# Local attention probabilities of batches 3 to 7 turned by 32x32 block transfers and VectorE instead of TensorE, in a new order of steps

## The chip, the cores and the metric

The kernel runs on one core of a Trainium2 chip. The metric is the device time of one execution in microseconds; the time before is 602.74 us, the median of three runs (602.57 to 603.37). One further execution was taken with the hardware profiler on; its page and trace are what is read below. Engines are named as in the profile: PE is TensorE (matmul), PEld its weight loads, DVE is VectorE, ACT is ScalarE, POOL is GpSimd, SP is SyncE, which here only issues DMA transfers.

## The reference

Eight batches, eight heads, 576 positions, head dimension 64. Two attentions are added and the sum goes through a feed-forward layer:

```python
# pooled: q, k, v averaged over groups of 4 positions, full softmax attention on 144 positions,
# the result repeated 4 times
out_up = np.repeat(sm_attn(q_d, k_d, v_d), 4, axis=2)
# local: each position sees only positions closer than 4
mask = np.abs(pos[:, None] - pos[None, :]) < 4
scores = np.where(mask, scale * np.matmul(q, k.transpose(0, 1, 3, 2)), -1e9)
out_local = np.matmul(softmax(scores), v)
x = (out_up + out_local) as 4608 tokens x 512
# feed-forward
h = x @ w_in                      # 512 -> 1024
solu = h * softmax(h)
ln = (solu - mean) / sqrt(var + 1e-6) * g_ln
return ln @ w_out                 # 1024 -> 512
```

Everything is computed in float32; the weights come as float64 and are converted on the chip.

## The kernel before

**Feed-forward.** The 4608 tokens are 36 tiles of 128. Both matmuls of a tile are done in a split of each operand into a high and a low part, three products per block: `ffn_in` (L770) issues 24 matmuls of 128x512, `ffn_out` (L888) another 24. `xhl` makes the parts of the input (`xh` on ACT at L919, `xl` on POOL at L922). Between the two matmuls stand the maximum (DVE, L778), the exponential (ACT, L782), the product with its sum (DVE, L785), the subtraction of the mean (ACT, L807), the square sum (ACT, L822) and some small POOL steps. To turn the 128x1024 result so that its columns lie on partitions, it is stored to a scratch tensor in memory (`u`, L813), read back in 32-row blocks (`v`, four transfers at L845), and transposed in 32x32 blocks by DVE (L866). ACT then makes `uh` (L872) and POOL (DVE for the last tiles) makes `ul` (L874).

**Local attention.** A batch's 576 positions are covered by ten windows of 64 rows, handled two at a time: five units (`Local`, u = 0 to 4) in each of eight batches, 40 in all. In `by_tensor`, which all 40 use, a unit goes through eleven steps: the scores of four head pairs (PE, L614: 16 products of 64x64, in the profile two records each), the mask added on the way out of PSUM into `pl` (DVE, L632), the row maximum (DVE, L637), its subtraction (POOL, L639), the exponential (ACT, L641), the row sum and its reciprocal (DVE, L644 and L648), the multiplication by it (POOL, L650), four 128x128 transposes of `pl` into PSUM (PE, L660), their copy to `plT` in SBUF (ACT, L663), the products with the values `vw` (PE, L670), and the write into `x` (L496 ACT for batches 1 to 7, L498 DVE for batch 0). `vw` comes by four transfers per unit (L264).

A second method, `by_blocks` (L515), is in the text and unused, because `ON_TENSOR = 8`. It lays `pl` out so that a later 32x32 block transpose is enough: eight transfers of 32 rows by 1 KB bring the blocks to their places in `plT` (L569), one DVE transpose of 128x512 turns them (L575), and the products read `plT` directly. Its values come by two transfers per unit, and its row sum is followed by a small DVE addition of 1e-9 (128x8).

**Pooled attention.** Per batch four head pairs (`Pooled`): scores (PE, L696), maximum (DVE, L703), exponentials (ACT, L711), reciprocal (DVE, L718), multiplication (POOL, L720), transposes (PE, L731), two copies (ACT L738; DVE L743 from batch 2 on, ACT before), products (PE, L752), addition to `x` (DVE, L498). The pooled values are summed on POOL (`pooled_vsum`, L434 and L437).

**Order.** All work is cut into 2099 numbered steps (generators that yield between instructions, collected in `plan`). `ORDER` at the top of the file lists the numbers in the order in which the steps are emitted, and each engine executes its own in that order. A tile that a step writes or reads makes the engines wait for one another; a DMA transfer makes the engine that issues it wait for its data. The first stretch also holds the conversion of the weights (`Weights`, L323 to L362, mainly DVE) and 24 pairs of matmuls on zeros (`keep_clock`).

Of the kernel before, what the change touches and what calls it, by code (L numbers as in the profile page):

```python
# [10 lines left out]
F32 = mybir.dt.float32  # L11
# [118 lines left out]
def pooled_local_attention_then_solu_ffn(  # L130
# [11 lines left out]
    P = 128  # L142
# [358 lines left out]

    ON_TENSOR = 8

    class Local:

# [534 lines left out]
```

## Time and profile before

| | |
|---|---|
| median of three runs | 602.74 us |
| profiled execution: its own time / its span | 602.74 us / 601.0 us |
| busy PE / PEld | 574.8 / 447.1 us |
| busy DVE / ACT / POOL | 396.5 / 361.8 / 375.6 us |
| share of the 16 DMA engines' time | 63.3% |
| moved | 94.34 MB in 203,913 packets |

The span runs from the first to the last instruction; the 1.74 us by which the execution's time exceeds it lie around it. "Busy" is the time in which at least one instruction of the engine ran, so overlapping instructions count once. A group's row gives the number of instructions, their busy time, the mean duration of one in ns, then the idle time just before them and who ended it. The chain of waits is followed back from the last instruction and gives each piece of the span to the engine or line that set it.

### The profile page before, as it was taken

To read this page: it belongs to the slowest core of one execution; us is meant where nothing else is said; L and a number is where in the kernel's file an instruction comes from. 1 tells how busy PE (TensorE), PEld (TensorE's weight loads), DVE (VectorE), ACT (ScalarE), POOL (GpSimd) and SP (SyncE) were. 2 spreads that over 40 slices of the span, in tenths; PEclk is the share of its full clock that TensorE was granted. 3 is DMA by queue.
4 is the path that set the end of the run, shared out by engine and by line. 5 is a ranking of instruction groups with operands and counts; after the bars stand their busy time and mean duration, and the time that the engine had idled before them with its cause. 6 is when DMAs were issued, how large, how long until landed. Compare 5 with 4: busy or idle time off the path is not lost.

```text
span 601.0 us, 15341 instructions
## 1 busy us (share of the span) xinstructions
PE 574.8 (96%) x5912; PEld 447.1 (74%) x5912; DVE 396.5 (66%) x692; ACT 361.8 (60%) x800; POOL 375.6 (62%) x553
## 2 busy tenths in 40 slices
PE   6889789899999999999999999999999999999996
PEld 3666557677777777787877777777777878788785
DVE  5989999869747677766856767737655533643541
ACT  3758866577745566566664854657465655553443
POOL 2576668867784778678574777656786767332221
PEclk8979999899999999999999999999999999999999
DMA  8999776687769767766878567847416623124230
GB/s 231 238 251 254 140 183 146 164 178 162 195 144 189 171 167 186 170 148 175 190 151 201 143 173 182 185 114 195 97 59 188 146 89 114 63 88 151 96 123 35
DMA packets 203913, 94.34 MB, mean 157 GB/s; under 512 B 162496, under 2 KB 192704, under 8 KB 203840
## 3 DMA queue, kind: packets, MB, share of 16 engines
q1 hardware_dynamic: 203840, 93.37, 63.3%
q8 instruction: 46, 0.75, 0.6%
q14 instruction: 27, 0.22, 0.1%
HBM read 65.54 MB, written 27.79 MB: 155 GB/s over the span
## 4 chain that ended last, share of the span: by engine, by line
PE 75%; POOL 6%; DVE 5%; ACT 4%; SPq 4%; DMA 3%; issue 3%; POOLq 0%; DVEq 0%
PE o L888 31%; PE h L770 27%; PE xp L670 3%; PE plt L660 3%; PE po L752 3%; PE sc L614 2%; DMA qm<-in_q_dram 2%; SPq L245 2%; PE pdt L731 2%; PE sd L696 2%; POOL pl L639 2%; DMA v<-u 1%; SPq L264 1%; POOL pd L720 1%; DVE w L334 1%
## 5 line engine op out<-in xcount | busy, mean ns | idle before, releaser
L888 PE MATMUL o<-wo_h,uh 128*128 128x512 f32 x288 | 117.9, 409 | 0.8 <-ACT uh L872 0.7
L770 PE MATMUL h<-wi_h,xh 128*128 128x512 f32 x288 | 116.3, 404 | 0.6 <-DVE e L785 0.6
L770 PE MATMUL h<-wi_h,xl 128*128 128x512 f32 x288 | 114.3, 397 | 1.3 <-POOL xl L922 1.3
L888 PE MATMUL o<-wo_l,uh 128*128 128x512 f32 x288 | 114.5, 398 | 0.0
L770 PE MATMUL h<-wi_l,xh 128*128 128x512 f32 x288 | 114.1, 396 | 0.0
L874 POOL TENSOR_TENSOR ul<-v,uh 128x512 fp32r<-128x512 f32 x58 | 74.4, 1288 | 19.7 <-ACT uh L872 7.7
L778 DVE TENSOR_REDUCE nmx<-h 128x1 f32<-128x1024 f32 x36 | 43.9, 1219 | 63.8 <-PE h L770 63.8
L888 PE MATMUL o<-wo_h,ul 128*128 128x512 f32 x288 | 79.1, 396 | 0.4 <-DVE ul L874 0.4
L782 ACT ACTIVATE e<-h,nmx 128x1024 f32<-128x1024 f32 x36 | 40.0, 1112 | 51.0 <-DVE nmx L778 51.0
L888 PEld LDWEIGHTS o<-wo_h,uh 128*128 128x128 f32 x288 | 54.6, 190 | 15.6 <-ACT uh L872 1.4
L770 PEld LDWEIGHTS h<-wi_h,xl 128*128 128x128 f32 x288 | 54.2, 188 | 15.2 <-POOL xl L922 2.1
L770 PEld LDWEIGHTS h<-wi_h,xh 128*128 128x128 f32 x288 | 54.2, 188 | 14.8 <-issue 1.0
L888 PEld LDWEIGHTS o<-wo_h,ul 128*128 128x128 f32 x288 | 54.2, 188 | 14.0 <-DVE ul L874 0.8
L770 PEld LDWEIGHTS h<-wi_l,xh 128*128 128x128 f32 x288 | 54.3, 189 | 12.2
L888 PEld LDWEIGHTS o<-wo_l,uh 128*128 128x128 f32 x288 | 54.5, 189 | 11.8
L922 POOL TENSOR_TENSOR xl<-x,xh 128x512 fp32r<-128x512 f32 (+1 forms) x40 | 47.1, 1183 | 18.6 <-ACT xh L919 17.4
L807 ACT ACTIVATE e<-e,nmu 128x1024 f32<-128x1024 f32 x35 | 40.1, 1146 | 28.2 <-POOL nmu L790 28.1
L785 DVE SCALAR_TENSOR_TENSOR e<-h,e 128x1024 f32<-128x1024 f32 x36 | 43.7, 1214 | 19.9 <-ACT e L782 19.9
L650 POOL TENSOR_TENSOR pl<-pl,rsl 128x512 f32<-128x512 f32 x40 | 42.1, 1055 | 20.7 <-DVE rsl L648 18.2
L866 DVE STREAM_TRANSPOSE v<-v 128x512 f32<-128x512 f32 x70 | 46.3, 688 | 12.5 <-DMA v<-u 12.5
L872 ACT ACTIVATE uh<-v 128x512 fp32r<-128x512 f32 x70 | 42.9, 623 | 14.9 <-DVE v L866 11.0
L639 POOL TENSOR_TENSOR pl<-pl,mxl 128x512 f32<-128x512 f32 x40 | 41.8, 1052 | 9.0 <-DVE mxl L637 4.6
(95 smaller groups left out, 1076.1 us busy)
## 6 DMA issues: line engine op xcount, KB each, us to landing
u<-e SPq DMA_DIRECT2D x35, 512.0 KB
v<-u SPq DMA_DIRECT2D x140, 128.0 KB
vw<-in_v_dram SPq DMA_DIRECT2D x160, 64.0 KB
vs<-in_v_dram SPq DMA_DIRECT2D x32, 288.0 KB
out_dram<-osb SPq DMA_DIRECT2D x36, 256.0 KB
qm<-in_q_dram SPq DMA_DIRECT2D x96, 72.0 KB
km<-in_k_dram SPq DMA_DIRECT2D x96, 72.0 KB
w<-in_moe_w_out_dram SPq DMA_DIRECT2D x8, 512.0 KB
```

The source lines that it names most:

```text
L639: nc.gpsimd.tensor_tensor(out=pl, in0=pl, in1=max_bc, op=ALU.subtract)
L650: nc.gpsimd.tensor_tensor(out=pl, in0=pl, in1=rs.unsqueeze(3).broadcast_to([P, NPR, 2, W]), op=ALU.mult)
L770: nc.tensor.matmul(hps[:, n, :], src[:, cc, :], wt[:, cc, n * 512:(n + 1) * 512], start=(cc == 0 and src is xh and wt is wi_h), stop=(cc = ...
L778: nc.vector.tensor_reduce(out=nmx, in_=hf, op=ALU.max, axis=AX.X, negate=True)
L782: nc.scalar.activation(e, hf, AF.Exp, bias=nmx, scale=1.0, accum_out=se)
L785: nc.vector.scalar_tensor_tensor(out=e, in0=hf, scalar=1.0, in1=e, op0=ALU.mult, op1=ALU.mult, accum_out=su)
L807: nc.scalar.activation(e, e, AF.Identity, bias=nmu, scale=1.0)
L866: nc.vector.transpose(vg, vg)
L872: nc.scalar.activation(uh, tp, AF.Copy)
L874: (nc.vector if v is None or i in LATE else nc.gpsimd).tensor_tensor(out=ul, in0=tp, in1=uh.bitcast(F32), op=ALU.subtract)
L888: nc.tensor.matmul(o, src[:, j, :], wt[:, 4 * g + j, :], start=(g == 0 and j == 0 and src is uh and wt is wo_h), stop=(g == 1 and j == 3 a ...
L922: nc.gpsimd.tensor_tensor(out=l, in0=src, in1=h.bitcast(F32), op=ALU.subtract)
```

## The change

`ON_TENSOR` becomes 3: the 15 local units of batches 0 to 2 keep `by_tensor`, the 25 of batches 3 to 7 go through `by_blocks`. In it, the four transfers of one window are issued by SP and the four of the other by ACT, as two steps of their own, so that a unit has twelve steps and the plan 2124.

A list `OTHER` names 121 steps that run on another engine than their usual one:

- from POOL to DVE: 18 of the `ul` steps, 17 of the `xl` steps, 8 of the 32 pooled value sums, 13 of the 32 pooled multiplications, 2 subtractions and 3 multiplications of local units in batches 1 and 2, 5 low parts of weights
- from ACT to DVE: the write into `x` of 16 local units (4 in batch 2, 2 in batch 3, 4 in batch 4, 1 in batch 5, 5 in batch 6), 9 first pooled copies and 1 second one, 7 of the subtractions of the mean, 1 `plT` copy in batch 2
- from DVE to ACT: 17 of the second pooled copies
- from DVE to POOL: the clamping of 4 weight pieces

`ORDER` is a new list throughout. The other edits add options that are switched off (`SUMS_ON_PE`, `G_LATE`, `FIRST_ON_PE`) or rename things; with `MASKED = 0` the new `stop` condition has the same value as before.

```diff
 ORDER = """
-181 0 182 1 2 3 165 25 183 166 4 5 6 184 167 185 24 26 186 187 188 27 7 8 173 32 168 169 170
+10 9 14 165 5 166 167 168 13 3 173 25 174 175 24 169 170 176 177 171 172 181 182 32 22 26 27
...
 """
+OTHER = """
+63 68 88 172 204 207 212 231 247 276 279 292 294 440 517 520 534 578 584 628 641 681 697 702
...
+"""
+    other = {int(n) for n in OTHER.split()}
+    now = [None]
+    def engine(usual, instead):
+        return instead if now[0] in other else usual
...
-    ON_TENSOR = 8
+    ON_TENSOR = 3
...
             plT = wk.tile([P, 2, H, 32], F32, tag="plT", name=f"plT_{b}_{u}")
-            for wi in range(2):
+            for wi, queue in enumerate((nc.sync, nc.scalar)):
                 for a in range(2):
                     for c in range(2):
-                        nc.sync.dma_start(
+                        queue.dma_start(
                             plT[wi * 64 + c * 32:][0:32, a].rearrange("q h k -> q (h k)"),
                             pl[wi * 64 + a * 32:][0:32, c * H * 32:(c + 1) * H * 32],
                         )
-            yield
+                yield
             flat = plT.rearrange("p a h q -> p (a h q)")
             nc.vector.transpose(flat, flat)
...
-            nc.gpsimd.tensor_tensor(out=l, in0=src, in1=h.bitcast(F32), op=ALU.subtract)
+            engine(nc.gpsimd, nc.vector).tensor_tensor(out=l, in0=src, in1=h.bitcast(F32), op=ALU.subtract)
...
     for n in ORDER.split():
-        fn, args = plan[int(n)]
+        now[0] = int(n)
+        fn, args = plan[now[0]]
         fn(*args)
```

The remaining places at which an engine is chosen by `engine(...)` are written in the same way.

More of the change, by code (lines that the diff above doesn't have):

```diff
@@ L208, in pooled_local_attention_then_solu_ffn, with make_bands @@
         nc.vector.tensor_copy(out=mask_b, in_=mask)
-    if WARM:
-        zeros = cpool.tile([P, P], BF16, name="zeros")
-        nc.gpsimd.memset(zeros, 0.0)
+    if MASKED:
+        filler = ident_b
+    elif WARM:
+        filler = cpool.tile([P, P], BF16, name="filler")
+        nc.gpsimd.memset(filler, 0.0)
     mhalf = cpool.tile([P, 1], F32, name="mhalf")
     nc.vector.memset(mhalf, -0.5)
+    GR = SD // 2
+    BAND = {0: (0, 16), 1: (3, 15), 3: (1, 15)}
+    bands = {}
+    def make_bands():
+        t = moe.tile([P, DFF], F32, tag="e", name="bands")[:, 0:3 * 160]
+        t = t.rearrange("p (r x) -> p r x", r=3)
+        nc.gpsimd.memset(t, 0.0)
+        by_half = ident.rearrange("p (h k) -> p h k", h=2)
+        for n, (r, (off, m)) in enumerate(BAND.items()):
+            nc.vector.tensor_reduce(
+                out=t[:, n, GR:GR + m],
+                in_=by_half[:, :, off:off + FAC * m].rearrange("p h (j i) -> p j h i", i=FAC),
+                op=ALU.add, axis=AX.XY,
+            )
+            bands[r] = t[:, n]
     LP = 2 * W + 2
@@ L233, in small_bank @@
     def small_bank(b, n):
-        return (ps_o, "o") if b < 2 and n % 2 and not W_PSUM and not WARM else (ps_t, "t")
+        return (ps_o, "o") if b < 2 and n % 2 and not WARM else (ps_t, "t")
     def load_q_k(t, b, pr):
@@ L433, in pooled_vsum, with pool_steps @@
             vs = self.vs.pop((c, hs.start))
-            nc.gpsimd.tensor_tensor(
+            eng = engine(nc.gpsimd, nc.vector)
+            eng.tensor_tensor(
                 out=vs[:, :, 0:2 * D], in0=vs[:, :, 0:2 * D], in1=vs[:, :, 2 * D:4 * D], op=ALU.add
             )
-            nc.gpsimd.tensor_tensor(
+            eng.tensor_tensor(
                 out=self.vd[:, c, hs], in0=vs[:, :, 0:D], in1=vs[:, :, D:2 * D], op=ALU.add
             )
+        def pool_steps(self):
+            firsts = [-(-s0 // FAC) for s0 in starts]
+            ends = firsts[1:] + [SD]
+            for c in range(2):
+                tp = two_banks(ps_h, "h", f"vp_{self.b}_{c}")[0:GR]
+                at = tp.rearrange("p h (r a d) -> p h r a d", r=NPR, a=2)
+                ws = range(5 * c, 5 * c + 5)
+                for w in ws:
+                    s0, g0, g1 = starts[w], firsts[w], ends[w]
+                    at0 = GR - (g0 - GR * c)
+                    K = FAC * g1 - s0
+                    for half in range(2):
+                        nc.tensor.matmul(
+                            at[:, half, :, half ^ (w % 2), :],
+                            bands[s0 % FAC][half * W:half * W + K, at0:at0 + GR],
+                            self.vw[w // 2][half * W:half * W + K, w % 2],
+                            start=w == ws[0], stop=w == ws[-1],
+                        )
+                yield
+                vd = self.vd[:, c].rearrange("p h d -> p (h d)")
+                nc.scalar.activation(vd, tp[:, 0], AF.Copy)
+                yield
+                nc.vector.tensor_tensor(out=vd, in0=vd, in1=tp[:, 1], op=ALU.add)
+                yield
     class EarlyBatch(Batch):
@@ L483, in pair_steps @@
                 yield
[L484 removed]
+                copy(
+                    engine(nc.scalar, nc.vector),
                     dst.rearrange("x (p a t) -> x p a t", a=2, t=HT),
[L486 removed]
+                    tp[:, :, 0:n].rearrange("x a (t p) -> x p a t", t=HT),
                 )
@@ L495, in accumulate @@
         if first:
-            nc.scalar.activation(x, part, AF.Copy)
+            copy(engine(nc.scalar, nc.vector), x, part)
         else:
             nc.vector.tensor_tensor(out=x, in0=x, in1=part, op=ALU.add)
-    ON_TENSOR = 8
+    ON_TENSOR = 3
     class Local:
@@ L616, in by_tensor @@
                         bt.qT[rows(par), pr, s0:s0 + W], bt.kT[rows(par), pr, s0:s0 + W],
-                        start=not early, stop=True,
+                        start=not early, stop=not early or pr == NPR - 1,
                     )
@@ L662, in by_tensor @@
             plT = wk.tile([P, NPR, 2, W], F32, tag="plT", name=f"plT_{b}_{u}")
-            nc.scalar.activation(plT, pt, AF.Copy)
+            copy(engine(nc.scalar, nc.vector), plT, pt)
             yield
@@ L737, in steps @@
             yield
-            nc.scalar.activation(pdT[:, :, :, 0, :], pt[:, 0], AF.Copy)
+            copy(engine(nc.scalar, nc.vector), pdT[:, :, :, 0, :], pt[:, 0])
             yield
-            if b < 2:
-                nc.scalar.activation(pdT[:, :, :, 1, :], pt[:, 1], AF.Copy)
-            else:
-                nc.vector.tensor_copy(out=pdT[:, :, :, 1, :], in_=pt[:, 1])
+            copy(
+                engine(nc.scalar, nc.vector) if b < 2 else engine(nc.vector, nc.scalar),
+                pdT[:, :, :, 1, :], pt[:, 1],
+            )
             yield
@@ L806, in ffn_in @@
         else:
-            nc.scalar.activation(e, e, AF.Identity, bias=nmu, scale=1.0)
+            if engine(nc.scalar, nc.vector) is nc.scalar:
+                nc.scalar.activation(e, e, AF.Identity, bias=nmu, scale=1.0)
+            else:
+                nc.vector.tensor_scalar(
+                    out=e, in0=e, scalar1=1.0, scalar2=nmu, op0=ALU.mult, op1=ALU.add
+                )
         s = small.tile([P, 1], F32, tag="s", name=f"s_{i}", bufs=6)
@@ L940, in pooled_local_attention_then_solu_ffn @@
     weights = Weights()
-    idle = []
     def keep_clock(n):
-        if not idle:
-            idle.append(ps_o.tile([P, 512], F32, tag="o", name="warm"))
+        o = ps_o.tile([P, 512], F32, tag="o", name=f"warm_{n}")
         for _ in range(2):
             nc.tensor.matmul(
-                idle[0].rearrange("p (a n) -> p a n", n=P), zeros,
-                zeros.unsqueeze(1).broadcast_to([P, 4, P]), start=True, stop=True,
+                o.rearrange("p (a n) -> p a n", n=P), filler,
+                filler.unsqueeze(1).broadcast_to([P, 4, P]), start=True, stop=True,
             )
@@ L981, in attention @@
     def attention(bt):
-        values(bt)
-        local = [Local(bt, u, bt.b > 0) for u in range(5)]
-        pooled = [Pooled(bt, pr, bt.b == 0) for pr in range(NPR)]
-        for it in pooled + local if bt.b == 0 else local + pooled:
-            if isinstance(it, Local):
+        by_pe = bt.b < SUMS_ON_PE
+        late = bt.b == 0
+        local = [Local(bt, u, not late) for u in range(5)]
+        pooled = [Pooled(bt, pr, late) for pr in range(NPR)]
+        if by_pe:
+            if not bt.b:
+                step(make_bands)
+            for u in range(5):
+                step(bt.load_v, u)
+            row(bt.pool_steps(), 6)
+        else:
+            values(bt)
+        for it in pooled + local if late else local + pooled:
+            if isinstance(it, Local) and not by_pe:
                 step(bt.load_v, it.u)
-            row(it.steps(), 10 if isinstance(it, Pooled) or bt.b < MASKED else 11)
+            row(it.steps(), 10 if isinstance(it, Pooled) or bt.b < MASKED else 11 + (bt.b >= ON_TENSOR))
     tiles = 0
```

43 lines of the change are left out of this document (31 added, 12 removed), and 203 rows, old and new, of tables (ORDER, OTHER).

## Prediction

> **What bounds the kernel now.** I read the page's busy times and slices first, to see which engine is full and when.
>
> ```profile
> span 601.0 us, 15341 instructions
> PE 574.8 (96%) x5912; PEld 447.1 (74%) x5912; DVE 396.5 (66%) x692; ACT 361.8 (60%) x800; POOL 375.6 (62%) x553
> PE   6889789899999999999999999999999999999996
> DVE  5989999869747677766856767737655533643541
> ```
>
> PE is full from the tenth slice on, DVE before that. Cut at the first matmul of tile 0's second product (95.9 us) and at that of tile 27 (504 us), the table of windows reads (length, then PE, PEld, DVE, ACT, POOL busy, PE clock, DMA share, GB/s):
>
> ```profile
> 0.00:62.90 62.90, 50.88 (x862) 36.36 (x862) 52.09 (x94) 41.10 (x106) 33.63 (x41) 0.92 0.98 238
> 62.90:95.90 33.00, 27.64 (x389) 20.55 (x383) 32.29 (x55) 24.20 (x53) 24.52 (x26) 1.00 0.74 167
> 95.90:135.90 40.00, 37.43 (x497) 29.17 (x492) 33.14 (x56) 26.06 (x59) 30.15 (x44) 0.96 0.76 162
> ...
> 95.90:504.00 408.10, 404.31 (x4193) 318.06 (x4188) 271.60 (x479) 249.95 (x560) 290.71 (x422) 1.00 0.66 158
> 504.00:601.00 97.00, 91.93 (x490) 72.16 (x480) 40.53 (x66) 46.59 (x83) 26.70 (x67) 1.00 0.29 95
> ```
>
> Up to 95.9 us PE idles 17.4 us (95.9 - 50.88 - 27.64) while DVE is 98% busy from 62.9 on. From 95.9 to 504 us PE idles only 3.8 of 408.1 us, and every other engine has a quarter of its time free or more. The chain of waits says the same of the whole span, by line:
>
> ```profile
> PE 75%; POOL 6%; DVE 5%; ACT 4%; SPq 4%; DMA 3%; issue 3%; POOLq 0%; DVEq 0%
> PE o L888 31%; PE h L770 27%; PE xp L670 3%; PE plt L660 3%; PE po L752 3%; PE sc L614 2%; DMA qm<-in_q_dram 2%; SPq L245 2%; PE pdt L731 2%; PE sd L696 2%; POOL pl L639 2%; DMA v<-u 1%; SPq L264 1%; POOL pd L720 1%; DVE w L334 1%
> ```
>
> So time taken from PE behind 95.9 us is worth its full length, as long as the other engines still deliver in time.
>
> **The change, part by part.** First what PE loses: the L660 transposes of 25 of 40 units.
>
> ```profile
> L660 PE MATMUL plt<-ident,pl 128*128 128x128 f32 x160 | 26.5, 290 | 3.1 <-ACT plT L663 3.1
> L614 PE MATMUL sc<-kT,qT 64*64 64x64 f32 x1280 | 27.5, 225 | 2.3 <-DVE pl L632 1.4 <-issue 0.9
> L670 PE MATMUL xp<-plT,vw 64*64 64x58 f32 x1024 | 21.8, 226 | 0.3 <-ACT pd L711 0.3
> ```
>
> The chain gives L660 3% of 601 us, 18 us for 40 units or 0.45 us each: 25 x 0.45 = **11.3 us**. Lower end: in the timeline the next matmul starts 0.41 us after a unit's first transpose, which gives 10.3.
>
> ```profile
> 329.36 0.66 PE L660 MATMUL plt<-ident,pl 128*128 128x128 f32 x4
> 329.77 0.47 PE L770 MATMUL h<-wi_h,xh 128*128 128x512 f32 x1
> ```
>
> Upper end: the group's busy time, 26.5/40 x 25 = 16.6, which counts overlap with neighbours. I take the chain's value, since it is what the end is made of. The value products become 64 columns wide instead of 56 or 58; L614 at 64 columns takes 225 ns against 226, so that costs nothing on PE.
>
> Next what the other engines gain and lose:
>
> ```profile
> L663 ACT ACTIVATE plT<-plt 128x512 f32<-128x512 f32 x40 | 23.6, 590 | 7.7 <-PE plt L660 7.6
> L866 DVE STREAM_TRANSPOSE v<-v 128x512 f32<-128x512 f32 x70 | 46.3, 688 | 12.5 <-DMA v<-u 12.5
> L648 DVE RECIPROCAL rsl<-sml 128x8 f32<-128x8 f32 x40 | 8.1, 203 | 1.9
> L874 POOL TENSOR_TENSOR ul<-v,uh 128x512 fp32r<-128x512 f32 x58 | 74.4, 1288 | 19.7 <-ACT uh L872 7.7 <-issue 3.0 <-DMA qm<-in_q_dram 2.3
> L874 DVE TENSOR_TENSOR ul<-v,uh 128x512 fp32r<-128x512 f32 x12 | 9.0, 765 | 7.6 <-ACT uh L872 5.5 <-issue 2.1
> L498 DVE TENSOR_TENSOR x<-x,xp 128x464 f32<-128x464 f32 x4 | 2.5, 624 | 0.4 <-PE xp L670 0.4
> L434 POOL TENSOR_TENSOR vs<-vs 72x512 f32<-72x512 f32 x32 | 41.4, 1293 | 0.6
> L437 POOL TENSOR_TENSOR vd<-vs 72x256 f32<-72x256 f32 x32 | 23.8, 742 | 2.5
> L720 POOL TENSOR_TENSOR pd<-pd,rsd 128x432 f32<-128x432 f32 x32 | 29.1, 913 | 9.8 <-DVE rsd L718 8.3 <-DMA out_dram<-osb 1.3
> L650 POOL TENSOR_TENSOR pl<-pl,rsl 128x512 f32<-128x512 f32 x40 | 42.1, 1055 | 20.7 <-DVE rsl L648 18.2 <-DVE r L816 1.4 <-DMA km<-in_k_dram 0.9
> L807 ACT ACTIVATE e<-e,nmu 128x1024 f32<-128x1024 f32 x35 | 40.1, 1146 | 28.2 <-POOL nmu L790 28.1
> L496 ACT ACTIVATE x<-xp 128x464 f32<-128x464 f32 x28 | 15.3, 555 | 17.7 <-PE xp L670 17.5
> L738 ACT ACTIVATE pdT<-pdt 72x288 f32<-72x288 f32 x32 | 12.7, 399 | 20.4 <-PE pdt L731 20.4
> L743 DVE COPY pdT<-pdt 72x288 f32<-72x288 f32 x24 | 10.6, 444 | 14.5 <-ACT pdT L738 14.5
> L785 DVE SCALAR_TENSOR_TENSOR e<-h,e 128x1024 f32<-128x1024 f32 x36 | 43.7, 1214 | 19.9 <-ACT e L782 19.9
> L325 DVE TENSOR_SCALAR w<-w 128x512 f32<-128x512 f32 x16 | 12.9, 814 | 5.6 <-ACT w L323 5.6
> ```
>
> DVE gets 25 block transposes at 688 ns (17.2 us) and 25 small additions, at most 203 ns each by L648; I take 0.1, 2.5 us. From POOL come 18 + 17 + 5 subtractions of 128x512 at 765 ns (30.6), 8 pooled sums, two additions each, together about 1.15 by their sizes (72x512 and 72x256) against that row (9.2), 13 pooled multiplications of 128x432 at about 0.58 (7.5) and 5 local ones at 0.68 (3.4). From ACT come 16 writes into x at about 0.6 by L498 (9.6), 10 pooled copies at 444 ns (4.4), 1 plT copy (0.7), and 7 mean subtractions over 1024 columns, between 0.69 and 1.21 by L866 and L785, taken as 1.0 (7.0). Off DVE go 17 copies at 444 ns (7.5) and 4 clamps at 814 (3.3). Sum: 17.2 + 2.5 + 50.7 + 21.7 - 10.8 = **81 us of DVE**, all but a few of them between the two cuts. L866's 70 x 688 = 48.2 are 46.3 busy, so 81 become some 78 busy: 271.6 + 78 = **350 us of DVE in a stretch that would last 408.1 - 11.3 = 396.8 us, 88%**, where it was 67%. It hides behind PE only if DVE can be kept that full; that is the open point of this change. A lower price for the pooled sums and mean subtractions takes at most 5 us off it.
>
> POOL loses 40 x 1.29 + 8 x (1.29 + 0.74) + 13 x 0.91 + 5 x 1.05 = 85 us, gets some 5 back with the clamps, and is nowhere near a bound. ACT loses 25 copies at 590 ns (14.8), and by the swaps 16 x 0.56 + 7 x 1.15 + 10 x 0.40 + 0.59 - 17 x 0.40 = 15 us, and gains 100 DMA issues. What an issue costs stands in SP's timeline, 1.75 and 2.74 us for four:
>
> ```profile
> 316.88 1.75 SPq L845 DMA_DIRECT2D v<-u  x4
> 319.46 0.34 SPq L813 DMA_DIRECT2D u<-e  x1
> 319.89 2.74 SPq L264 DMA_DIRECT2D vw<-in_v_dram  x4
> ```
>
> By the first, whose row blocks are the nearest, 100 issues are 44 us on ACT: 249.95 - 29 + 44 = 265 of 397 us, hidden behind PE. By the second they are 69 and ACT is at 290, hidden still. SP gets 44 as well and loses 50 of its vw issues at 0.69 (34). Each set of four waits for the POOL multiplication of its unit: on SP the q, k and v loads and the scratch stores queue behind it, on ACT everything ACT does. In the new list PE has over 2 us of work between the multiplication and the first issue in 14 of 25 units, there nothing is held; in the other 11 it has at most half a us, and the issuing engine may stand for one multiplication, 1.05 us by L650. On SP, whose loads come long before their use, I price that at nothing; on ACT it would be 12 us in all of the 107 that are left free.
>
> How long the transfers take no row shows; the nearest is the scratch read, four transfers of 128 KB, in the chain of waits:
>
> ```profile
> 318.20 5.45 DMA v<-u
> ```
>
> Eight transfers of 32 KB should land in no more than that behind the same traffic, and not below zero. Adding up PE's work in the new list between the last issue of a unit and its value products gives 5.6 to 27 us, for 22 of 25 units above 7. So the transfer and the 0.69 us of transpose fit, and I price them at nothing; the cover gone, each us missing in each unit is 25 us. The 6.6 MB are 7% on 94.34 MB at a DMA share of 0.66.
>
> [...]
>
> The start. In the new list DVE has, by the rows, as much work before tile 0's second product as in the old one (98 against 99 us by means), so with DVE at 98% there I expect 95.9 us again: 0. The tail keeps its order of events: 0. Renamings, the switched-off options and the new warm-up tile add no instruction: 0.
>
> Last, PE's idle time with DVE at 88%. The stretch 62.9 to 95.9 had DVE at 98% and PE idle for 5.4 of 33 us, 95.9 to 135.9 DVE at 83% and PE idle for 2.6 of 40, the rest at 65% almost nothing. Bounds: 0, and 6.4% of 397, 25 us. Those early windows also wait for weights and first loads, and later steps can run far ahead, so I take 1%, **4 us**.
>
> Sum, against the profiled execution's own 602.74 (span 601.0 and 1.74 around it, the same as the median): 602.74 - 11.3 + 4 = **595.4 us**.
>
> **Rivals.**
>
> *The forecast*: PE bounds, with a few more stalls; 589 to 600. Chance 0.52.
>
> *A better order as well*: the swaps shorten chains, stalls stay at 3.8 us, and the start gets shorter. For: before tile 0's first matmul the new list has 59.5 us of DVE work where the old one has 65, so it may come 5 us earlier. Against: by tile 0's second product that lead is used up. 602.74 - 11.3 - 5 = 586.4. Chance 0.15.
>
> *DVE becomes the bound* from 95.9 to 504 us, slower than before. Place: the maxima at L778 and the block transposes stand in one DVE queue with all that was moved there, and PE waits for both. The point from which it decides: 350 us need more than 350/409 = 85.6% of DVE to end no later than now. For: 83% is the most it reached after the start. Against: 98% at 62.9 to 95.9. At 83% the stretch lasts 422 us, 13.5 more: 616. Chance 0.21, a third of it between the forecast and that.
>
> *The transfers come late* or ACT is held at its issues. For: the wait of 5.45 us and SP's queue, shared with the loads. Against: the cover counted above. Half a us missing per unit takes the gain back: 602.74 - 11.3 + 12.5 = 604. Chance 0.12.
>
> That the change does not act is excluded: the twelve steps match the generator, and 60 of 160 L660 transposes remain.
>
> **How the numbers follow.** A difference under 0.2% (1.2 us) can't be told from none. Faster: 0.50 of the forecast, 0.15, 0.03 from the last two: 0.68. Same: 0.02, 0.06 of DVE's case near 85.6%, 0.03: 0.11. Slower: 0.13 and 0.08: 0.21. The range reaches from 585 to 606: below lies little of the better order, above DVE's case at 83%. The forecast's own is 589 to 600.
>
> **What would show it.** L660 with 60 transposes and 7 us less in the chain; DVE between 465 and 480 us busy, about 88% in the middle stretch; POOL near 300. PE's idle time there, 3.8 now, tells the forecast (up to 10) from DVE's case (above 15, with PE's matmuls of L770 and L888 released by DVE). If the value products L670 wait for the transposes of plT, and these for DMA, the transfers are late. I am wrong if PE's chain share does not fall or the start moves by more than 5 us.

## The result and the profile after

The changed kernel takes 625.89 us (median of four runs, 622.21 to 628.72), against 603.06 us for the kernel before on the same chip (602.57 to 604.32): a ratio of 1.037, 95% interval 1.031 to 1.043. Forecast were 595.4 us and a range of 585 to 606. The profiled execution took 623.39 us, its span is 621.5. The page of the changed kernel begins so (PEclk is the granted clock in 40 slices of the span, in tenths):

```profile
span 621.5 us, 15495 instructions
PE 572.8 (92%) x5812; PEld 438.9 (71%) x5812; DVE 483.0 (78%) x830; ACT 334.3 (54%) x758; POOL 319.0 (51%) x482
PEclk9989998999999899998999999999999999999999
```

The busy times are near what was expected, though above it: DVE 483.0 (465 to 480 forecast), POOL 319.0 (near 300). PE is no more than 2.0 us less busy than before, though 100 transposes are gone. The groups that answer to the priced rows (line, engine, operation, shapes, count, busy us, mean ns, idle before):

```profile
L746 PE MATMUL plt<-ident,pl 128*128 128x128 f32 x60 | 10.2, 296 | 1.6 <-POOL pl L736 1.4 <-ACT plT L267 0.3
L664 PE MATMUL xp<-plT,vw 64*64 64x64 f32 x800 | 18.2, 227 | 0.0
L659 DVE STREAM_TRANSPOSE plT<-plT 128x512 f32<-128x512 f32 x25 | 17.3, 691 | 1.7 <-DMA v<-u 1.6
L642 DVE TENSOR_SCALAR sml<-sml 128x8 f32<-128x8 f32 x25 | 7.1, 285 | 0.9
```

The block transpose costs 691 ns (688 forecast) and never waits for its transfers: 1.6 of its 1.7 us of idle time were ended by another tile's data. The small addition costs 285 ns where I had put 100. By stage, cut at the same events as in the prediction (first matmul of the second product of tile 0 and of tile 27), the table of windows reads (length, then PE, PEld, DVE, ACT, POOL busy, clock, DMA share, GB/s):

```profile
0.00:99.79 99.79, 78.98 (x1269) 55.65 (x1269) 93.00 (x156) 64.68 (x151) 59.05 (x62) 0.97 0.88 209
99.79:533.14 433.35, 410.37 (x4152) 317.54 (x4153) 350.50 (x612) 233.59 (x547) 240.49 (x364) 0.98 0.68 165
533.14:621.50 88.36, 83.42 (x393) 65.76 (x391) 39.47 (x63) 36.09 (x61) 19.50 (x56) 1.00 0.29 96
```

The start takes 3.9 us more than before. The new order leaves 8.5 us less of PE's work for the last stage (83.42 against 91.93), so the last two stages are added: before, 505.1 us with PE busy 496.24 and idle 8.9; now 521.71 us with PE busy 493.79 and idle 27.9. So the 20.5 us by which the span grew are 3.9 at the start, 19.1 of PE's idle time behind it, and 2.5 less work. DVE's 350.50 us in the middle stage are what the prediction had (350), but they fill only 81% of it.

PE's idle time is no longer spread thin. Its table of waits (us in total, times, longest) begins:

```profile
PE o L980 <- ACT uh L963: 8.0, 3, 4.9
PE sd L782 <- ACT pd L797: 4.6, 2, 4.1
PE pdt L817 <- POOL pd L806: 4.5, 1, 4.5
```

Three waits, at 212.48, 293.12 and 369.76 us, take 4.1 to 4.9 us each. I followed each back. The second, in the timeline of ACT (start, length; in brackets the idle time and what ended it):

```profile
281.31 0.69 ACT L987 ACTIVATE osb<-o,s 128x512 f32<-128x512 f32 x1 [0.34 <-PE o L980]
287.91 3.16 ACTq L653 DMA_DIRECT2D plT<-pl  x4
291.11 0.41 ACT L267 ACTIVATE pdT<-pdt 72x288 f32<-72x288 f32 x1 [9.11 <-DMA plT<-pl]
291.42 1.14 ACT L894 ACTIVATE e<-e,nmu 128x1024 f32<-128x1024 f32 x1
292.45 0.62 ACT L963 ACTIVATE uh<-v 128x512 fp32r<-128x512 f32 x1
```

ACT can do nothing but the next thing in its list, four transfers of `plT`. It stands 5.9 us before the first can be issued, needs 3.16 us from there to the end of the fourth, and only then makes the copy, the subtraction and the `uh` for which PE waits. What it stands for is not its own operand: the first issue, at 287.91, starts 0.02 us behind the landing of a store that SP issued at 280.06 and that writes another tensor:

```profile
280.06 0.34 SPq L904 DMA_DIRECT2D u<-e  x1
```

The third PE wait has four issues that take 7.26 us from 359.47 on, of which they issue for 2.19 us and stand between them for the rest; the first has four that begin at 207.81 after 3.8 us of standing, 0.08 us behind the landing of a load of `v` that SP issued at 202.54. On PE, the clock comes on top (timeline, then windows of one us):

```profile
287.62 0.40 PE L856 MATMUL h<-wi_l,xh 128*128 128x512 f32 x1
287.85 0.39 PE L856 MATMUL h<-wi_h,xl 128*128 128x512 f32 x1
293.12 0.79 PE L980 MATMUL o<-wo_h,uh 128*128 128x512 f32 x1 [4.88 <-ACT uh L963]
293.71 0.63 PE L980 MATMUL o<-wo_l,uh 128*128 128x512 f32 x1
294.14 0.63 PE L980 MATMUL o<-wo_h,uh 128*128 128x512 f32 x1
```

```profile
293.00:294.00 1.00, 0.88 (x2) 0.78 (x3) 0.38 (x1) 1.00 (x3) 0.85 (x1) 0.50 0.93 284
...
297.00:298.00 1.00, 1.00 (x4) 0.71 (x4) 1.00 (x3) 0.80 (x1) 0.18 (x1) 0.50 0.16 24
...
299.00:300.00 1.00, 1.00 (x5) 0.77 (x5) 1.00 (x3) 0.00 (x0) 0.19 (x1) 1.00 0.82 201
```

For the five us from 293 to 298 the granted clock is 0.50, and a matmul of 128x512 that started 0.23 us after the one before now starts 0.43 us after it. By half the time at half clock, an estimate, the wait of 4.88 us costs about 2.6 us more in this way (5.2 us at 0.50); those at 212 and 370 cost 1.7 each (3.41 us at 0.50 from 212.97 and from 369.98 on). That is a large part of why PE's busy time fell so little. A shorter wait of this run was followed by the same: behind the 2.41 us that PE waits at 99.79 the clock is 0.50 for 3.4 us (100.33 to 103.74).

What an issue costs, by the view of the tile `plT` (ns, min/median/max; first and last start), and what ACT's idle time ended with, by its table of waits:

```profile
L653 ACTq DMA_DIRECT2D plT<-pl x100: 514/602/2020, 190.5 to 516.3; - x100
L653 SPq DMA_DIRECT2D plT<-pl x100: 507/589/1867, 191.4 to 517.7; - x100
```

```profile
ACT pdT L267 <- DMA plT<-pl: 20.1, 4, 9.1
ACT mxd L793 <- DMA plT<-pl: 14.4, 2, 7.5
```

Added up issue by issue, ACT's 100 issues take 63.3 us, 0.63 each in the mean: between the prediction's two prices (44 and 69 us), though the longest takes 2.02. On top of that ACT stands 31.9 us at them, 12.2 ahead of the first of four and 19.7 between the four, where the prediction allowed 12. Of these 31.9 us, 27.6 were ended by the landing of an older transfer of SP (17 issues, each starting 0.02 to 0.08 us behind the landing), and only 1.1 of those by one of SP's `plT` transfers: the rest were SP's loads and stores (8.1 `vs`, 6.3 `u`, 5.4 `vw`, 5.4 `v`, 1.2 the output, 0.2 `km`).

### The profile page after: what moved, and what is told of

Its sections match the earlier page's. It is cut to its first block, busy times and chain, and to the rows that moved or that the text cites. A ratio compares the mean times of both kernels' runs of the same rounds, so it can differ in the third digit from the quotient of the medians.

```text
span 621.5 us, 15495 instructions
## 1 busy us (share of the span) xinstructions
PE 572.8 (92%) x5812; PEld 438.9 (71%) x5812; DVE 483.0 (78%) x830; ACT 334.3 (54%) x758; POOL 319.0 (51%) x482
## 5 line engine op out<-in xcount | busy, mean ns | idle before, releaser
L980 PE MATMUL o<-wo_h,uh 128*128 128x512 f32 x288 | 120.0, 417 | 9.7 <-ACT uh L963 8.0
L856 PE MATMUL h<-wi_h,xh 128*128 128x512 f32 x288 | 117.6, 408 | 0.7 <-DVE e L871 0.4
L980 PE MATMUL o<-wo_l,uh 128*128 128x512 f32 x288 | 116.5, 405 | 0.0
L966 POOL TENSOR_TENSOR ul<-v,uh 128x512 fp32r<-128x512 f32 x40 | 52.8, 1323 | 63.8 <-ACT uh L963 36.4
L980 PEld LDWEIGHTS o<-wo_h,uh 128*128 128x128 f32 x288 | 55.7, 193 | 26.5 <-ACT uh L963 9.2
L980 PEld LDWEIGHTS o<-wo_l,uh 128*128 128x128 f32 x288 | 55.8, 194 | 12.2
L856 PEld LDWEIGHTS h<-wi_l,xh 128*128 128x128 f32 x288 | 54.6, 190 | 11.9
L868 ACT ACTIVATE e<-h,nmx 128x1024 f32<-128x1024 f32 x36 | 39.9, 1110 | 41.4 <-DVE nmx L864 37.5
L894 ACT ACTIVATE e<-e,nmu 128x1024 f32<-128x1024 f32 x28 | 32.1, 1147 | 25.6 <-POOL nmu L876 19.0
L987 ACT ACTIVATE osb<-o,s 128x512 f32<-128x512 f32 x36 | 24.6, 682 | 38.2 <-PE o L980 16.2
L646 POOL TENSOR_TENSOR pl<-pl,rsl 128x512 f32<-128x512 f32 x25 | 27.4, 1097 | 29.6 <-DVE rsl L644 25.5
L876 POOL TENSOR_SCALAR nmu<-su 128x1 f32<-128x1 f32 x36 | 8.4, 233 | 59.0 <-DVE e L871 51.3
```

Of the source, the lines that this page charges most:

```text
L646: nc.gpsimd.tensor_tensor(out=by_head, in0=by_head, in1=of_head(rs), op=ALU.mult)
L856: nc.tensor.matmul(hps[:, n, :], src[:, cc, :], wt[:, cc, n * 512:(n + 1) * 512], start=(cc == 0 and src is xh and wt is wi_h), stop=(cc = ...
L868: nc.scalar.activation(e, hf, AF.Exp, bias=nmx, scale=1.0, accum_out=se)
L876: nc.gpsimd.tensor_scalar(out=nmu, in0=su, scalar1=-1.0 / DFF, scalar2=0.0, op0=ALU.mult, op1=ALU.add)
L894: nc.scalar.activation(e, e, AF.Identity, bias=nmu, scale=1.0)
L966: (usual if v is None else engine(usual, nc.vector)).tensor_tensor(out=ul, in0=tp, in1=uh.bitcast(F32), op=ALU.subtract)
```

## The experiments

The expectations name theories. A, and later Q: ACT is held at its issues, because it waits there for others' transfers. T: the time of the issues alone is the loss. D: DVE is too full. O: the new order and the other engines of 121 steps lose by themselves. G: GpSimd has too much.

| run | us (runs) | ratio to before, 95% |
|---|---|---|
| changed kernel | 625.89 (4) | 1.037, 1.031 to 1.043 |
| all transfers from SP | 629.01 (4) | 1.045, 1.040 to 1.050 |
| new order, TensorE | 622.71 (4) | 1.036, 1.030 to 1.042 |
| no step on another engine | 644.79 (4) | 1.071, 1.065 to 1.076 |
| SP and GpSimd issue | 608.62 (5) | 1.010, 1.006 to 1.014 |
| old order, TensorE, other engines | 636.92 (4) | 1.059, 1.055 to 1.064 |
| old order, 17 units by blocks, SP and GpSimd | 639.50 (4) | 1.062, 1.055 to 1.069 |
| the same with other engines | 664.32 (4) | 1.102, 1.096 to 1.108 |
| SP and GpSimd issue, copies on ACT | 615.08 (4) | 1.021, 1.018 to 1.024 |
| halves exchanged | 635.20 (4) | 1.054, 1.046 to 1.061 |
| old order, 17 units by blocks, SP | 644.73 (4) | 1.072, 1.064 to 1.079 |
| old start, SP and GpSimd issue | 609.45 (6) | 1.010, 1.007 to 1.013 |
| GpSimd and ACT issue | 620.29 (4) | 1.028, 1.025 to 1.032 |
| all transfers from GpSimd | 641.18 (4) | 1.063, 1.058 to 1.068 |

**All transfers from SP.**

```diff
-            for wi, queue in enumerate((nc.sync, nc.scalar)):
+            for wi, queue in enumerate((nc.sync, nc.sync)):
```

> The changed kernel with all eight transfers of a unit issued by SP; order, steps and swaps as they are. Theory A (ACT is held at its transfer issues, and PE then waits for what ACT has behind them): ACT loses 100 issues and the waits in front of them, the idle time of PE in the middle stretch falls from about 22 us to under 10 and the time to 600-612 us. Rival D (DVE is too full): DVE is unchanged, so the time stays at 618-630. Rival O (the new order and the swaps are bad by themselves): 618-630 too. If SP itself becomes the bound (100 more issues at 0.6 us and more), loads come late and the time rises above 630.

629.01 us: taking ACT out of it did not help, because now SP is late. In the waits of DVE and of PE:

```profile
DVE plT L659 <- DMA plT<-pl: 11.9, 6, 6.1
```

```profile
PE h L856 <- DVE e L871: 8.1, 6, 4.0
```

The transposes wait for their transfers, up to 6.1 us, what stands behind them on DVE waits too, and the next first product, which needs the PSUM that the step making `e` still reads, starts late.

**TensorE in the new order.** `ON_TENSOR = 8`; for batches 3 to 7 the transposes on PE and their copy stand together in the slot where ACT's four transfers stood, the slots of SP's transfers and of the block transpose are empty.

> The new order and swaps, but the 25 units turned by TensorE as before, the transposes and ACT's copy at the place where ACT's four transfers were issued. Gives PE back some 11 us, takes 20 us from DVE and all 200 transfers from SP and ACT. Theory A: the holding of ACT is gone, 606-616 us or less. Rival D: DVE falls from 88 to 83%, a part of the stalls goes, 612-622. Rival O: the time stays above 618, since order and swaps are unchanged.

622.71 us. So the new order and the other engines lose some 20 us with no block transfer at all; this is O's part. Windows of this kernel, middle and last stage (the start takes 99.67):

```profile
99.67:531.84 432.17, 415.39 (x4252) 323.26 (x4253) 332.38 (x562) 245.68 (x572) 238.64 (x364) 1.00 0.62 150
531.84:619.90 88.06, 83.44 (x393) 65.78 (x391) 39.38 (x63) 36.10 (x61) 19.51 (x56) 0.99 0.29 96
```

PE is idle 16.8 us in the middle stage, where the kernel before had 3.8, in many waits of at most 2.4 us. That need not be a price of the order for the change, though: the order was not made for these steps.

**No step on another engine** (`OTHER` empty, the rest as changed).

> The changed kernel with an empty list of swapped engines: 62 us of work go back from DVE, 80 us to POOL and 15 us to ACT, transfers as they are. Theory A: ACT is held as before and has more to do, 620-640 us. Rival D: with DVE near 70% again the stalls go and the time falls below 612. Rival O, if the swaps are what is bad: below 612 too.

644.79 us, 19 more than the changed kernel. Windows, middle stage:

```profile
100.02:556.91 456.89, 423.70 (x4152) 324.59 (x4153) 298.50 (x538) 243.72 (x559) 295.30 (x427) 0.95 0.64 157
```

DVE has 298.50 us of work here, 65% of the stage, and the stage is the longest of all: a DVE that is too full is not what makes the changed kernel slow. In this order the moved steps help.

**SP and GpSimd issue.**

```diff
-            for wi, queue in enumerate((nc.sync, nc.scalar)):
+            for wi, queue in enumerate((nc.sync, nc.gpsimd)):
```

> The changed kernel with ACT's four transfers of each unit issued by POOL instead. [...] Theory A: ACT is free, 600-614 us unless POOL's issue takes over 2 us each. Rivals D and O: 618-630, as DVE and order are unchanged.

608.62 us: 17 less than the changed kernel from one word. The three windows:

```profile
0.00:100.33 100.33, 79.60 (x1268) 56.64 (x1268) 93.13 (x156) 64.59 (x151) 59.07 (x62) 0.95 0.84 209
100.33:519.09 418.76, 406.35 (x4152) 314.17 (x4153) 356.00 (x612) 234.75 (x547) 293.02 (x464) 1.00 0.70 171
519.09:607.10 88.01, 83.44 (x393) 65.77 (x391) 39.39 (x63) 36.07 (x61) 19.52 (x56) 0.99 0.29 96
```

PE's idle time in the middle stage goes from 23.0 to 12.4 us, and its busy time by 4.0, with the clock back at 1.00: the long waits are gone. DVE is now 85% full there, more than in the changed kernel, and PE gets on. Beside the run with TensorE, in the same order, PE's busy time in the middle is 415.39 - 406.35 = 9.0 us less: that is what turning the 25 units away from PE is worth. The longest wait behind the start is 2.46 us long, at 354.80, and the clock does not fall behind it (timeline, windows):

```profile
354.80 0.53 PE L817 MATMUL pdt<-ident,pd 64*72 64x64 f32 x12 [2.46 <-POOL pd L806]
```

```profile
355.00:356.00 1.00, 1.00 (x45) 0.85 (x39) 0.96 (x3) 0.63 (x2) 1.00 (x2) 1.00 0.95 352
```

GpSimd as the second issuer is 17 us better than ACT, and not because the transfers are faster: from issue to landing the view of the tile `plT` gives 1.7/2.6/6.6 us here (min/median/max), and the landings in the trace of the changed kernel give medians of 2.3 for SP's half and 2.7 for ACT's. What differs is what stands at the issues and behind them: GpSimd is idle 6.4 us in all ahead of its 100 issues, where ACT stood 31.9.

**Old order, TensorE, other engines.** The changed kernel with `ON_TENSOR = 8`, the order of before, and `OTHER` naming the same 121 steps by their numbers in that plan.

> The order of the kernel before, with the transposes of all batches on TensorE as before; only the steps that the changed kernel gives to the other engine are given to it here too (VectorE some 62 us more by the tally of its rows, GpSimd some 80 less, ScalarE some 15 less). Theory O (the new order costs the 20 us that the run with TensorE in the new order lost, not the other engine of these steps): within 3 us of before, 599 to 605. Theory D (VectorE over 85% of the stretch holds the chain, in whatever order): 612 to 622, with PE's waits ended by VectorE.

636.92 us, beyond what either theory gave. The waits of PE in front:

```profile
PE h L861 <- DVE xl L1019: 3.8, 3, 2.1
PE sc L703 <- DVE qT L476: 3.7, 3, 1.8
```

In the order of before the moved steps lose 35 us, 11 of them at the start (the second product of tile 0 begins at 106.94 instead of 95.90); in the new order they win 19. An order and the engines of its steps belong together. The waits for DVE here come with DVE busy 468.7 us, 73% of the span, less than in the changed kernel, so I read them as a matter of where in its queue a step stands and not of how full DVE is.

**Old order, 17 units by blocks, SP and GpSimd.** Those of the 25 units that have 8.8 us or more of PE's work between multiplication and second product; the transfers stand at the place of PE's transposes or up to a few us ahead of it, and the block transpose 1.5 us of PE's work ahead of the second product. The added `memset` sets border values of `pl` again that a unit by blocks overwrites and a unit by TensorE sums.

```diff
+    BLOCKS = {(3, 0), (3, 2), (3, 4), (4, 0), (4, 1), (4, 2), (5, 0), (5, 1), (5, 3), (6, 0), (6, 1), (6, 2), (6, 3), (6, 4), (7, 0), (7, 1), (7, 3)}
-            return self.by_tensor() if self.bt.b < ON_TENSOR else self.by_blocks()
+            return self.by_blocks() if (self.bt.b, self.u) in BLOCKS else self.by_tensor()
...
+            if b >= 3:
+                nc.vector.memset(pl_all.rearrange("p (r x) -> p r x", x=LP)[:, :, 0:LP:LP - 1], 1e-9)
```

> The order of the kernel before, no step on another engine; 17 of the 25 units of batches 3 to 7, those with 8.8 us or more of PE's work between their multiplication and their second product, are turned by blocks, transfers half from SyncE and half from GpSimd where PE's transposes stood, VectorE's transpose 1.5 us of PE's work ahead of the second product. The other 8 stay on TensorE. Theory O with Q (blocks are worth PE's time where no engine in the chain issues): PE loses 17 x 0.41 = 7.0 us, VectorE gains 17 x 0.97 = 16.5 us of slack work; 594 to 599. Theory D: VectorE's 16.5 us more show as waits of PE for VectorE, 602 to 612. Theory S (transfers of any queue come behind SP's and GpSimd's own waits, so the second product waits): 605 to 625, PE waiting in front of the second products.

In this kernel and the next, the transfers of batch 7's first unit read `pl` after another unit's masked scores were written to it, so that unit is computed from other values; the amount of work is the same. 639.50 us, above all three ranges: the order of before with 17 units by blocks loses 38 us. In front of PE stands POOL (waits of PE, then POOL's issues):

```profile
PE h L858 <- POOL xl L1016: 6.9, 5, 2.8
PE plt L748 <- POOL pl L738: 5.4, 2, 4.7
```

```profile
L653 POOL DMA_DIRECT2D plT<-pl x68 | 35.1, 521 | 10.2 <-PE xp L664 7.6 <-DVE pl L718 1.7 <-POOL pl L646 0.3
```

**The same with other engines.**

> As the run before this one (17 units by blocks in the order of before, transfers from SyncE and GpSimd), and the steps that the changed kernel gives to the other engine given to it here too: VectorE up to some 480 us. Theory O: the other engine of these steps does neither good nor harm in this order, 593 to 600, within 3 us of that run. Theory D: 610 to 625, slower than that run by 10 or more.

664.32 us, the slowest of all and above both ranges: of the two losses in the old order, 38 and 35 us, most adds up (62).

**SP and GpSimd issue, copies on ACT.**

```diff
-            for wi, queue in enumerate((nc.sync, nc.scalar)):
+            for wi, queue in enumerate((nc.sync, nc.gpsimd)):
...
+                if wi:
+                    for _ in range(13):
+                        nc.scalar.activation(scratch, scratch, AF.Copy)
                 yield
```

> The run with SyncE and GpSimd as issuers in the new order (608.62), and in the slot where ScalarE issued its four transfers 13 copies of 128x64 that wait for nothing, some 3 us per unit, about what four issues took of ScalarE (3.1 us), 75 us in all; their output is used by nothing. Theory Q (ScalarE's wait for the transfers of the other queue is what cost 17 us): 608 to 613. Theory T (the time of the issues on ScalarE alone costs it): 620 to 627, PE's waits for ScalarE back at over 4 us.

615.08 us, 6.5 more than without the copies, just above what Q gave and below T. In the middle stage ACT has 312.22 us of work instead of 234.75. These 77.5 us are 14 more than the 63.3 that the issues took of it in the changed kernel:

```profile
99.72:526.01 426.29, 411.11 (x4153) 316.80 (x4153) 354.19 (x611) 312.22 (x872) 292.67 (x463) 0.98 0.69 167
```

PE is idle 15.2 us in it. So the time of the issues alone, which I had priced at nothing, costs at most 6 to 7 of the 17 us; the other 10 come from something that the copies don't have, and the waits for landings are the one such thing that the trace of the changed kernel shows.

**Halves exchanged.**

```diff
-            for wi, queue in enumerate((nc.sync, nc.scalar)):
+            for wi, queue in enumerate((nc.scalar, nc.sync)):
```

The idea comes from the trace of the changed kernel, where 27.6 us of ACT's standing at its issues ended with a landing of SP's transfers. With the first half, ACT should have less of them ahead of it: forecast were waits at the issues that fall by a third or more from 65.6 us, and a time of 612 to 622 us.

> The changed kernel with the two halves exchanged: ScalarE issues the four transfers of the first half, SyncE those of the second, one step later in the order. [...] Rival (ScalarE waits for GpSimd's multiplication, or the time of the issues is all): 623 to 630.

635.20 us: a miss, slower by 9 instead of faster. ACT's idle time up to its issues' end grew from 65.6 to 72.2 us, added up over its waits, and SP, which now has the later half, waits longer for ACT (waits of SP; 39.9 us in the changed kernel):

```profile
SPq L904 <- ACT e L894: 46.1, 14, 9.5
```

Of ACT's standing at its issues, landings still ended 22.6 us (27.6 in the changed kernel). The exchange left most of these waits in place, so it is no test of what they cost.

**Old order, 17 units by blocks, SP.** As the run with SP and GpSimd, with `(nc.sync, nc.sync)`, and batch 7's first unit issued before its `pl` is written again.

> The order of the kernel before, no step on another engine, 17 of 25 units by blocks, all transfers from SyncE. Theory G (the run with half of them from GpSimd was slow because GpSimd, 410 us busy there, was late with its subtractions: PE waited 6.9 us for xl, 5.4 for pl, 4.2 for ul): 596 to 606, PE's waits for GpSimd gone. Theory O2 (any 17 units moved in an order that was fitted to the engines' times put it out of step, whichever queue): 620 to 640.

644.73 us, so G was not the cause; it is O2's case, even above its range. Windows, middle stage, and waits of DVE:

```profile
95.92:543.26 447.34, 416.14 (x4126) 323.52 (x4120) 287.00 (x521) 241.71 (x543) 290.98 (x423) 0.95 0.65 156
```

```profile
DVE pl L707 <- DMA plT<-pl: 10.5, 2, 5.5
DVE pl L617 <- DMA plT<-pl: 8.7, 2, 4.5
```

The start is that of before to 0.1 us, the last stage to 0.2 (96.84 us). The loss lies wholly where the units are, at 2.3 us for each of 17. DVE stands up to 5.5 us because the next use of a `pl` (L707 is the added `memset`, L617 the masked scores) waits until the transfers have read it; PE is idle 31.2 us and works at half clock for some 40 us of the 447, which by half of that, an estimate, costs some 20 us more.

**Old start, SP and GpSimd issue.** The first 671 steps in the order and on the engines of before, the rest as in the run with SP and GpSimd.

> The run with SyncE and GpSimd as issuers (608.62), but the steps up to the first scores of the fourth batch (671 of 2124) stand in the order of before and on the engines of before; the rest is the new order. Theory S4 (the new order's start costs the 4 us that all runs with it had lost at the first product of the first tile): that product starts near 96 instead of 100.3, and the time is 603 to 606. Rival (the start's loss is made up for later, the two parts don't fit): 607 to 615.

609.45 us. The first matmul of tile 0's second product comes at 95.38 instead of 100.33, and the gain is lost again in the next stage:

```profile
95.38:517.66 422.28, 407.74 (x4184) 316.29 (x4177) 346.36 (x603) 235.41 (x542) 298.48 (x476) 0.99 0.71 171
```

422.28 us against 418.76. The rival held: the two parts don't fit, and the 4 us at the start are not to be had by themselves.

**GpSimd and ACT issue** (`(nc.gpsimd, nc.scalar)`).

> The changed kernel with the first half of the transfers issued by GpSimd in place of SyncE, the second half by ScalarE as in it. ScalarE's issues stay (some 78 us in all), but the four transfers of the same unit that stood ahead of them in the common order of SyncE and ScalarE are gone, and SyncE is not held for them. Theory Q (what the 13 copies of 128x64 did not show of the 17 us is ScalarE's wait for SyncE's transfers): ScalarE's idle time ahead of its issues falls from 14 us to under 5, and the time to that of the copies, 611 to 619. Rival (the issues' own time, up to 2 us each, is longer or comes at worse places than the copies): 622 to 630.

620.29 us, between the two forecasts. ACT's standing at its issues, added up as above, falls only from 31.9 to 18.8 us (ahead of the first of four from 12.2 to 5.7), what landings ended of it from 27.6 to 11.6; the issues themselves take 62.9 us, as before. What is left can be seen in the timelines of SP and ACT:

```profile
221.64 0.40 SPq L320 DMA_DIRECT2D vs<-in_v_dram  x1
222.14 2.75 SPq L303 DMA_DIRECT2D vw<-in_v_dram  x4
```

```profile
223.75 0.51 ACTq L653 DMA_DIRECT2D plT<-pl  x1
227.57 4.03 ACTq L653 DMA_DIRECT2D plT<-pl  x3
231.65 0.41 ACT L267 ACTIVATE pdT<-pdt 72x288 f32<-72x288 f32 x1 [7.63 <-DMA plT<-pl]
```

ACT issues one transfer and stands until 227.57, though all four need the same multiplication. The second of the four starts 0.02 us behind the landing, at 227.55, of SP's load of `vs` issued at 221.64. The three issues that follow, at 227.57, 228.74 and 231.09, take 0.51 to 0.52 us each; the last two stood until loads of `vw` had landed. So taking SP's half away left SP's loads and stores, which hold ACT as well. The rival, longer issues, is out: their sum has not changed. By the ratios, of the 16 us between ACT and GpSimd as the second issuer 5.3 are gone in this run, at most 6.6 are the time of the issues, and some 4.5 are left beside that, with 11.6 us of waiting for landings left. That the parts add up so is an assumption, and no run took these waits alone away.

**All transfers from GpSimd** (`(nc.gpsimd, nc.gpsimd)`).

> All eight transfers of a unit from GpSimd in the new order. GpSimd has 100 issues of 0.53 us more than where it issued half (371.6 us busy there): some 424 us. Theory G (GpSimd has the room, SyncE's loads and stores come earlier): 602 to 608. Rival (GpSimd's 4.2 us per unit hold its multiplications, PE waits for pd and pl): 610 to 620.

641.18 us, beyond the rival's range. POOL's issues, and the first of PE's waits:

```profile
L653 POOL DMA_DIRECT2D plT<-pl x200 | 101.4, 513 | 7.1 <-issue 3.2 <-POOL pl L646 2.2 <-POOL pd L806 0.7
```

```profile
PE o L980 <- POOL ul L966: 7.1, 3, 3.5
```

Another 49 us of issues on an engine that was busy 61% of the time, where SP had issued these transfers, cost 32 us of the whole.

## Why the prediction was wrong

**The step that failed** is "100 DMA issues on ACT ... hidden behind PE", with "on ACT it would be 12 us in all of the 107 that are left free". ACT does have the room (233.59 us busy in 433), but room over a stage hides nothing where PE waits for that engine's next instruction within a us or two. The issues' own time was priced well (63.3 us measured, 44 to 69 forecast), but it is not hidden: it costs up to 6 to 7 us of the whole (copies in their place). The wait at the issues was mis-sized and put down to the wrong thing: ACT stood 31.9 us at them, not 12, in pieces of up to 5.9 us, not 1.05, and 27.6 of these us ended with the landing of older transfers, nearly all SP's loads and stores (26.5), not with the multiplication. I had looked for the wait at the tile alone, and in the kernel before it could not hold ACT, since only SP issued there; on SP its trace has such waits, one of 0.2 us inside the row of `vw` that the prediction shows, ended 0.02 us behind the landing of a load of `vs`. The rival "ACT is held at its issues" was the right mechanism with too small a price (604 us) and chance.

ACT's part is 17 of the 30 us between the forecast and the result. The run with SP and GpSimd issuing is still 13 us above the forecast: 4.4 at the start, 4.1 of PE's idle time behind it and 4.9 of PE's work, which fell there by 6.4 us and not by 11.3. The next terms are these.

**What a long wait costs** was no term at all. All 21 waits of PE of 3.3 us and more that the traces of this case have behind their first 5 us are followed by 2.9 us or more at a granted clock of 0.50; the sum had PE's idle time at its length only. By half the time at 0.50, an estimate, it is some 6 us in the changed kernel and some 20 in the run with 17 units by blocks from SP.

**PE loses 11.3 us**: mis-sized. In the same order it is 9.0 us of busy time; against the kernel before it is 6.4, since PE is 2.6 us busier behind the start in the new order with TensorE (498.8 against 496.2), for a reason that no run shows. The value products, priced at nothing, are part of the difference: 800 of them are 18.2 us busy, where 800 at the rate of before (21.8 for 1024) were 17.0.

**PE idle + 4 us**: in the best run with blocks in this order, SP and GpSimd issuing, it is 12.4 in the middle stage against 3.8, so + 8.6 without any long wait, and + 19 in the changed kernel. The row that I scaled by (DVE at 83%, PE idle 6.4%) gave 25 as the bound, nearer than my value.

**The start: 0.** It is 3.0 to 5.7 us in all runs with the new start; equal amounts of DVE work do not make equal times. Undone alone, it brought nothing, so as a term of the sum it was wrong and as a cause it is none.

**DVE becomes the bound**: not borne out. DVE had 350.50 us of work, the forecast amount, and at 85% of a shorter stage PE went on. With 65% DVE (no step on another engine) the time was worse.

**The transfers**, priced at nothing: held, in the changed kernel. Its block transpose waited for none. From SP alone it waited 11.9 us. What the transfers cost is not their landing but eight issues per unit, and the waits at them, on lists that have other things to do (63.3 us of issues and 31.9 of standing on ACT in the changed kernel).

Put together, as spans: before 601.0; new order and other engines with TensorE 619.9 (+ 18.9); blocks in place of TensorE, SP and GpSimd issuing, 607.1 (- 12.8); ACT in place of GpSimd 621.5 (+ 14.4). The first is not a cost of its own, since no part of the change was found to work without the others: the old order with the moved steps, with the blocks, or with both is 35 to 62 us slower than before; the new order alone, with TensorE and no moved step, was not run. Why the best combination still stands 1% above the kernel before is open; its idle time in the middle is made of waits under 2.5 us for ACT, POOL and DVE.

## What to carry to other kernels

In a program whose engines each follow a fixed list, price an added transfer not by the issuing engine's free time but by what stands behind it in its list and by everything its issue was seen to stand for in a trace (27.6 of ACT's 31.9 us here ended with landings of SP's older transfers); and try each issuer: of the six ways that were run here, half from SP and half from GpSimd was the fastest and all from GpSimd the slowest. A long wait of PE can cost more than its length: look at the granted clock behind it (the 4.88 us here cost an estimated 2.6 us more, at 0.50). An order that was fitted to its steps is part of every one of them: try a change of an engine or a path together with a new order, since in an old one even removed work can lose.

## What was not expected of the hardware

The issue of one transfer of 32 KB took ACT 0.51 to 2.02 us and SP 0.51 to 1.87 in the changed kernel (medians 0.60 and 0.59), and GpSimd 0.51 to 0.53 us in the mean of each of the seven runs in which it issued. Four on ACT took 7.26 us from the start of the first to the end of the last, 2.19 of them issuing; two of them stood for 1.65 and 3.38 us and started 0.02 us behind the landing of a load of SP (`vw`, `vs`). PE's granted clock was 0.50 for 2.9 us or more behind each of the 21 waits of 3.3 us and more (all traces, the first 5 us of each left out). Of the 52 waits between 2.0 and 3.3 us, 41 were followed by it too, such as 2.46 us at 109.30 of the kernel before, and 11 were not, such as 2.46 us (SP and GpSimd issuing, at 354.80), 2.74 (GpSimd and ACT, at 417.52) and 3.17 (all from GpSimd, at 459.42). The stretches at 0.50 inside the spans of the kernel before and the changed kernel were 3.4 us long five times and 6.8 us three times. A 128x512 float32 block transpose on VectorE, from SBUF in place, took 0.691 us for `plT` in the changed kernel and 0.688 for the row blocks in the kernel before.
